# Gate sums in two parts, the rounding's integer add on VectorE, the first squares on ScalarE, and another order of the first loads in an mLSTM + squared-ReLU kernel

## The chip, the cores, the metric

One core of one Trainium2 chip. The metric is the device time of one execution in microseconds (us). Times are medians; the profile is one execution, some 2 us shorter than its time because it counts from the first to the last instruction.

## The reference, cut to what matters

```python
# 1. mLSTM cell: batch 4 x 8 heads, 768 steps, head width 40
for t in range(S):
    m_new  = maximum(f_gate[t] + m, i_gate[t])          # running maximum
    f_stab = exp(f_gate[t] + m - m_new)
    i_stab = exp(i_gate[t] - m_new);  m = m_new
    C = f_stab * C + i_stab * outer(v[t], k[t])
    n = f_stab * n + i_stab * k[t]
    y[t] = sigmoid(o_gate[t]) * (C @ q[t]) / maximum(abs(n . q[t]), 1)
# 2. y becomes x: (3072 tokens, 320)
# 3. feed-forward: w_in (320, 2048), w_out (2048, 320), given in float64
h   = maximum(x @ w_in, 0)
out = (h * h) @ w_out
```

## The kernel before

The cell is computed in 24 steps of 128 time steps (six for each batch). The gates are summed along time by scans on VectorE (`do_gates`), giving `A_sb` (sums of log f) and `i_sb` (called b). For each step, `A_bc` (the sums, spread over 128 partitions, masked on GpSimd) goes through exponentials on ScalarE into the weights `W_sb`; TensorE makes scores, VectorE multiplies them by `W_sb` (`weighted`), TensorE forms `hi`, `dC`, `hp` (`attend`), VectorE puts them together (`num`, `normalise`), and TensorE turns the rows into `xT` (`turn_rows`), the input of the feed-forward.

The weights `w_in` and `w_out` arrive as float64. Each of 26 pieces is rounded to FP32 on the chip in two steps, words on ScalarE and a join on VectorE and GpSimd:

```python
def words(self):                      # ScalarE; mag and low have two buffers each
    nc.scalar.activation(mag[:, :w], raw[:, :, 1].bitcast(F32), AF.Abs)              # L179
    nc.scalar.activation(low[:, :w], raw[:, :, 0].bitcast(U32), AF.Copy,
                         bias=2.0, scale=2.0 ** -51)                                  # L181
def join(self):                       # VectorE, and the last add on GpSimd
    nc.vector.tensor_scalar(mag, mag, ..., op0=ALU.max, op1=ALU.min)                  # L190
    nc.vector.tensor_scalar(bits, bits, scalar1=3, op0=ALU.logical_shift_left)        # L194
    nc.vector.scalar_tensor_tensor(bits, in0=self.raws[n][:, :w, 1], ...)             # L195
    nc.gpsimd.tensor_tensor(dst.bitcast(I32), bits, low.bitcast(I32), op=ALU.add)     # L199
    self.fetch()                      # the next raw piece, on the same queue as all loads
def step(self):                       # words run one piece ahead of joins
    if len(self.a) == len(self.b): self.words()
    self.words(); self.join()
```

The start, cut to the part that the argument touches (`A_bc` has two buffers, and `weigh_on(s)` issues the fetch for step s + 2):

```python
    do_gates()                        # all 768 columns at once
    ...
    rounding.words(); turn_gates(); rounding.join()
    weigh(0); transposes(1, ...); spread_A(1); scores(1, ...); weigh(1)
    weighted(0); weighted(1, spare=True)
    load(2); load_A(2)
    ...
    rounding.step(); load(3); load_A(3)
    turn_rows(0); idle(4); transposes(2); idle(4); turn_rows(1)
    rounding.step(); weigh_on(2)
```

Then steps 2 to 5 of the cell are overlapped with the first layer for the first 512 tokens, in eight turns u, each with one half group (24 matmuls, 4.5 us) on TensorE:

```python
    NEXT = (6, 8, 10, 12, 15, 18, 21, 24)      # joins done by the end of each turn
    for u in range(8):
        s = 2 + u // 2
        relu_half()
        if u % 2 == 0:
            ...                                 # scores(s), turn_rows(s-1), ffn1_half
            rounding.step(); weighted(s); weigh_on(s + 1); square_half()
        else:
            ...                                 # sigmoids where new o gates are needed
            attend(s); rounding.step(); normalise(s)
            transposes(s + 1); ffn1_half(0, u // 4, u % 4); square_half()
            ...                                 # loads
        while rounding.done < NEXT[u]: rounding.step()
```

After the loop, 497 us of the second layer and of the remaining groups follow, in which TensorE has hardly a gap (busy for 493.2 of 496.6 us).

## Time and profile before

| | before |
|---|---|
| time, median of 3 runs | 610.29 us (607.38 to 610.32) |
| profiled span, mean granted clock | 606.7 us, 0.989 |
| first half group of the first layer starts | 31.66 us |
| second half group ends (u = 0, 1) | 54.29 us |
| eighth half group ends (u = 2 to 7) | 108.53 us |
| second layer (L509) starts | 110.11 us |
| from there to the end | 496.6 us |

The five times in the middle were read from TensorE's timeline and the chain of work. They cut the span into stretches. In the profile's notation PE is TensorE, PEld its weight loads, DVE VectorE, ACT ScalarE, POOL GpSimd, SP the queue that issues the loads; "L199" is a line of the kernel. A bank is a buffer that TensorE writes its results to and that has to be read before it is filled again; a turn of the gates or of rows is their transposition by TensorE (the eight turns u of the loop are another thing). The prediction shows the lines themselves.

### The profile page before, as it was taken

How to read it: one execution, taken by the hardware profiler on the slowest of the kernel's cores; microseconds unless marked ns; L12 is line 12 of the kernel's file. 1: busy time of each engine (PE TensorE's matmuls, PEld its weight loads, DVE VectorE, ACT ScalarE, POOL GpSimd, SP SyncE). 2: the span in 40 equal slices, each digit the busy share in tenths (PEclk: the TensorE clock that was granted, in tenths of full speed). 3: DMA queues.
4: the chain of work that ended last, by engine and by line, in shares of the span. 5: the costliest groups of instructions: out<-in, count | busy, mean ns of one | idle time of the engine just before them, and what ended most of it. 6: DMA issues, size and time to landing. Idle time of an engine off the chain costs nothing.

```text
span 606.7 us, 7558 instructions
## 1 busy us (share of the span) xinstructions
PE 592.3 (98%) x2870; PEld 389.3 (64%) x2871; DVE 239.6 (39%) x468; ACT 192.4 (32%) x476; POOL 95.9 (16%) x113
## 2 busy tenths in 40 slices
PE   9979897999999999999999999999999999999997
PEld 5868776777645677645577655477755477733575
DVE  7688989712334322235323144322143431113100
ACT  3757567123351321132320524410214312022100
POOL 3345444202101110101021010101010110000000
PEclk9988998999999999999999999999999999999999
DMA  9898899615212143133143123122201000000000
GB/s 197 206 184 200 158 199 222 102 59 100 46 44 43 37 88 66 50 61 58 35 90 55 56 34 66 37 59 51 70 1 36 0 1 23 11 11 2 0 23 22
DMA packets 130901, 42.47 MB, mean 70 GB/s; under 512 B 101073, under 2 KB 127697, under 8 KB 130865
## 3 DMA queue, kind: packets, MB, share of 16 engines
q1 hardware_dynamic: 130768, 41.79, 33.2%
q8 instruction: 23, 0.38, 0.3%
q10 hardware_dynamic: 96, 0.20, 0.1%
q14 instruction: 14, 0.11, 0.1%
HBM read 37.95 MB, written 4.03 MB: 69 GB/s over the span
## 4 chain that ended last, share of the span: by engine, by line
PE 89%; DVE 6%; ACT 2%; issue 1%; POOL 1%; POOLq 0%; DVEq 0%; ACTq 0%
PE o_ps L509 35%; PE h_ps L452 23%; PE h_ps L457 7%; PE hp L392 6%; PE tp L355 3%; PE tp L342 3%; PE dC L385 3%; PE hi L378 2%; PE h_ps L476 2%; PE tp L437 1%; DVE mag L194 1%; DVE mag L195 1%; ACT W_sb L318 1%; PE idle L549 1%; POOL A_bc L312 1%
## 5 line engine op out<-in xcount | busy, mean ns | idle before, releaser
L509 PE MATMUL o_ps<-w_out,g 128*128 128x320 f32 x768 | 213.8, 435 | 0.0
L509 PEld LDWEIGHTS o_ps<-w_out,g 128*128 128x128 f32 x768 | 143.5, 190 | 57.9 <-issue 0.8
L452 PE MATMUL h_ps<-xT,w_in 128*128 128x512 f32 x320 | 146.9, 602 | 0.0
L461 DVE TENSOR_TENSOR g<-r_sb 128x512 f32<-128x512 f32 x80 | 51.7, 688 | 147.8 <-ACT r_sb L460 147.8
L452 PEld LDWEIGHTS h_ps<-xT,w_in 128*128 128x128 f32 x320 | 57.7, 190 | 69.9 <-issue 65.2
L460 ACT ACTIVATE r_sb<-h_ps 128x512 f32<-128x512 f32 x80 | 43.4, 595 | 162.6 <-PE h_ps L457 162.5
L515 ACT COPY y_sb<-o_ps 128x320 f32<-128x320 f32 x24 | 10.2, 425 | 185.8 <-PE o_ps L509 185.8
L318 ACT ACTIVATE W_sb<-A_bc,b_T 128x128 f32<-128x128 f32 x176 | 53.7, 391 | 7.9 <-POOL A_bc L312 7.9
L329 POOL TENSOR_TENSOR vw<-va,W_sb 128x328 f32<-128x328 f32 x20 | 14.9, 743 | 211.2 <-ACT W_sb L318 205.3
L367 DVE TENSOR_TENSOR P_sb<-tp,W_sb 128x512 f32<-128x512 f32 x46 | 29.6, 684 | 45.1 <-PE tp L355 43.0
L392 PE MATMUL hp<-va,P_sb 128*128 128x41 f32 x368 | 45.7, 286 | 0.0
L457 PE MATMUL h_ps<-xT,w_in 64*128 64x512 f32 x160 | 45.2, 641 | 0.0
L392 PEld LDWEIGHTS hp<-va,P_sb 128*128 128x128 f32 x368 | 44.6, 198 | 0.0
L346 DVE COPY qT<-tp 128x512 f32<-128x512 f32 x23 | 15.8, 687 | 70.2 <-PE tp L342 70.2
L411 POOL TENSOR_TENSOR C_sb<-C_sb,Cd 128x328 f32<-128x328 f32 x16 | 14.5, 906 | 138.1 <-DVE C_sb L403 137.8
L476 PE MATMUL h_ps<-xT,w_in 128*128 128x256 f32 x128 | 33.1, 415 | 3.0 <-ACT r_sb L495 1.2
L457 PEld LDWEIGHTS h_ps<-xT,w_in 64*128 64x128 f32 x160 | 12.0, 184 | 30.3 <-issue 30.3
L476 PEld LDWEIGHTS h_ps<-xT,w_in 128*128 128x128 f32 x128 | 26.1, 210 | 8.1 <-ACT r_sb L495 1.6
L355 PEld LDWEIGHTS tp<-qT,kT 40*128 40x128 f32 x384 | 24.1, 187 | 10.8 <-issue 6.8
L342 PE MATMUL tp<-ident,kq 128*128 128x128 f32 x192 | 26.6, 283 | 3.3 <-DVE num L398 3.3
L355 PE MATMUL tp<-qT,kT 40*128 40x128 f32 x384 | 27.1, 280 | 0.8 <-DVE qT L346 0.8
L342 PEld LDWEIGHTS tp<-ident,kq 128*128 128x128 f32 x192 | 23.0, 147 | 4.5 <-DVE num L398 3.8
(82 smaller groups left out, 468.8 us busy)
## 6 DMA issues: line engine op xcount, KB each, us to landing
A_bc<-a_rows SPq DMA_DIRECT2D x22, 512.0 KB, 3.9
raw<-in_moe_w_out_dram SPq DMA_DIRECT2D x16, 320.0 KB, 4.1
raw<-in_moe_w_in_dram SPq DMA_DIRECT2D x8, 512.0 KB, 5.1
kq<-in_k_dram SPq DMA_DIRECT2D x24, 160.0 KB, 4.0
kq<-in_q_dram SPq DMA_DIRECT2D x24, 160.0 KB, 4.4
va<-in_v_dram SPq DMA_DIRECT2D x24, 160.0 KB, 4.1
og<-in_o_gate_dram SPq DMA_DIRECT2D x24, 160.0 KB, 4.0
out_dram<-y_sb SPq DMA_DIRECT2D x24, 160.0 KB, 1.8
```

The costliest lines, as they stand in the source:

```text
L318: nc.scalar.activation(d["W"][:, i * n + h, :], A[i][:, h, :], AF.Exp, bias=b_T[:, b, c, i * n + h : i * n + h + 1],)
L342: nc.tensor.transpose(tp[:, j, :], d["kq"][:, i, 2 * j : 2 * j + 2, :].rearrange("p h d -> p (h d)"), ident[:],)
L355: nc.tensor.matmul(sc[i][:, j, :], lhsT=d["kT"][rows, j, :], rhs=d["qT"][rows, j, :], start=True, stop=True,)
L367: nc.vector.tensor_tensor(t, d["sc"][i], d["W"][:].rearrange("p (j two) t -> p j two t", two=2)[:, :, i, :], op=ALU.mult,)
L385: nc.tensor.matmul(dC[:, j].rearrange("p h d -> p (h d)"), lhsT=d["kq"][:, 0, 2 * j : 2 * j + 2, :].rearrange("p h d -> p (h d)"), rhs=d[" ...
L392: nc.tensor.matmul(hp[:, h, :], lhsT=d["P"][h % 2][:, h // 2, :], rhs=d["va"][:, h, :], start=True, stop=True,)
L452: nc.tensor.matmul(h[:], lhsT=w_in[:, a, fb * P : (fb + 1) * P], rhs=xT[:, a, :], start=(a == 0), stop=False,)
L457: nc.tensor.matmul(hs[i][:], lhsT=w_in2[rows, p, :], rhs=xT[rows, 2, :], start=False, stop=True)
L460: nc.scalar.activation(r[:], hs[i][:], AF.Relu)
L461: nc.vector.tensor_tensor(st["g2"][:, 2 * p + i, :], r[:], r[:], op=ALU.mult)
L476: nc.tensor.matmul(hs[i][:, n, :], lhsT=w_in[:, a, fb * P : (fb + 1) * P], rhs=xT[:, a, cols], start=(n == 0 and a == 0), stop=False,)
L509: nc.tensor.matmul(o_ps, lhsT=st["g2"][:, fb, j * P : (j + 1) * P], rhs=w_out[:, fb, :], start=(fb == 0), stop=(fb == NF - 1),)
```

## The change

Its intent: get the first gates sooner by summing 256 of 768 columns first; take the integer add off GpSimd, whose masks wait behind it; take the squares off VectorE; and order the first loads by need. Cut to its core:

```diff
-            nc.gpsimd.tensor_tensor(dst.bitcast(I32), bits, low.bitcast(I32), op=ALU.add)
+            nc.vector.tensor_tensor(dst.bitcast(I32), bits, low.bitcast(I32), op=ALU.add)
 ...
-    def do_gates():                    # scans, sums and b over all S columns
+    def do_gates(c0, c1):              # the same over columns c0*P to c1*P, carried on
+    def do_b(c0, c1):
-    def turn_gates():
+    def turn_gates(c0, c1):
 ...
-    def relu_half():                   # Relu on ScalarE, a turn later the square:
-                nc.vector.tensor_tensor(g4[:, :, i, :], r[:], r[:], op=ALU.mult)
+    def square_half():                 # Relu and square together, at the end of a turn
+                nc.scalar.activation(rs[-1][:], h[:], AF.Relu)
+                nc.scalar.activation(g4[:, :, i, :], r[:], AF.Square)
 ...
-    idle(4) ... idle(3) ... do_gates() ... turn_gates() ... weigh(0) ...
+    do_gates(0, 2); do_b(0, 2); spread_A(0); turn_gates(0, 2)
+    scores(0); weigh(0)
+    do_gates(2, NB)
+    nc.sync.dma_start(A_d[:, :], A_sb[:]); fetch(1); load_A(2)
+    rounding.words(); spread_A(1); transposes(1, (False, True))
+    weighted(0); scores(1, (True, True)); weigh(1)
+    do_b(2, NB)
+    rounding.step()
+    sigmoid(0); sigmoid(1)
+    attend(0); weighted(1, spare=True); normalise(0)
+    load(2)
+    turn_gates(2, NB)
+    attend(1)
+    rounding.step()
+    normalise(1)
+    load_o(2); load_o(3)
+    turn_rows(0); weigh_on(2); idle(4); transposes(2); turn_rows(1)
+    rounding.step()
+    load(3); load_A(3)
```

The cuts leave out the first loads (the three parts of step 0 now ahead of all raw weights), the removed idle matmuls (27 before, 16 after) and the place of `P` for step 1.

More of the change, by code (lines that the diff above doesn't have):

```diff
@@ L226, in load_gates @@
         nc.scalar.dma_start(i_sb[:], i_gate.rearrange("b h s -> (b h) s"))
-    def do_gates():
-        nc.vector.tensor_tensor_scan(m_sb[:], f_sb[:], i_sb[:], -1e30, op0=ALU.add, op1=ALU.max)
-        nc.vector.memset(f_sb[:, 0:1], 0.0)
-        nc.vector.tensor_tensor(f_sb[:, 1:], f_sb[:, 1:], m_sb[:, : S - 1], op=ALU.add)
-        nc.vector.tensor_tensor(f_sb[:, 1:], f_sb[:, 1:], m_sb[:, 1:], op=ALU.subtract)
-        nc.vector.tensor_scalar_max(f_sb[:], f_sb[:], LOG_ZERO)
+    def do_gates(c0, c1):
+        t0, t1 = c0 * P, c1 * P
+        now = slice(t0, t1)
@@ L234, in do_gates @@
         nc.vector.tensor_tensor_scan(
-            A_sb[:], keep[:].rearrange("p c t -> p (c t)"), f_sb[:], 0.0, op0=ALU.mult, op1=ALU.add,
+            m_sb[:, now], f_sb[:, now], i_sb[:, now], m_sb[:, t0 - 1 : t0] if c0 else -1e30, op0=ALU.add, op1=ALU.max,
         )
-        nc.vector.tensor_tensor(i_sb[:], i_sb[:], m_sb[:], op=ALU.subtract)
-        nc.vector.tensor_tensor(i_sb[:], i_sb[:], A_sb[:], op=ALU.subtract)
-    def turn_gates():
+        if c0 == 0:
+            nc.vector.memset(f_sb[:, 0:1], 0.0)
+            t0 = 1
@@ new lines, in do_gates @@
+        f, m = f_sb[:, t0:t1], m_sb[:, t0:t1]
+        nc.vector.tensor_tensor(f, f, m_sb[:, t0 - 1 : t1 - 1], op=ALU.add)
+        nc.vector.tensor_tensor(f, f, m, op=ALU.subtract)
+        nc.vector.tensor_scalar_max(f_sb[:, now], f_sb[:, now], LOG_ZERO)
+        nc.vector.tensor_tensor_scan(
+            A_sb[:, now], keep[:, c0:c1].rearrange("p c t -> p (c t)"), f_sb[:, now], 0.0, op0=ALU.mult, op1=ALU.add,
+        )
+    def do_b(c0, c1):
+        now = slice(c0 * P, c1 * P)
+        nc.vector.tensor_tensor(i_sb[:, now], i_sb[:, now], m_sb[:, now], op=ALU.subtract)
+        nc.vector.tensor_tensor(i_sb[:, now], i_sb[:, now], A_sb[:, now], op=ALU.subtract)
@@ L241, in turn_gates @@
+    def turn_gates(c0, c1):
         for src, dst in ((i_sb, b_T), (A_sb, eA_T)):
-            tp = ps_o.tile([P, W], F32, name="tp", tag="o_ps")[:, : S // P * BH].rearrange("p (c r) -> p c r", r=BH)
-            for c in range(NB):
-                nc.tensor.transpose(tp[:, c, :], src[:, c * P : (c + 1) * P], ident[:BH, :BH])
+            tp = ps_o.tile([P, W], F32, name="tp", tag="o_ps")[:, : (c1 - c0) * BH]
+            tp = tp.rearrange("p (c r) -> p c r", r=BH)
+            for c in range(c0, c1):
+                nc.tensor.transpose(tp[:, c - c0, :], src[:, c * P : (c + 1) * P], ident[:BH, :BH])
@@ L245, in turn_gates @@
             nc.scalar.activation(
-                dst[:].rearrange("p b c h -> p c b h"), tp.rearrange("p c (b h) -> p c b h", b=B),
+                dst[:, :, c0:c1, :].rearrange("p b c h -> p c b h"), tp.rearrange("p c (b h) -> p c b h", b=B),
                 AF.Copy if dst is b_T else AF.Exp,
@@ L362, in weighted @@
         d["P"] = []
+        if spare:
+            free = xts.tile([P, 3, W], F32, name="xT")
         for i in range(2):
-            t = ffn.tile([P, W], F32, name="r_sb", bufs=4) if spare else work.tile([P, W], F32, name="P_sb")
-            t = t[:].rearrange("p (j t) -> p j t", j=PR)
+            t = free[:, i] if spare else work.tile([P, W], F32, name="P_sb")[:]
+            t = t.rearrange("p (j t) -> p j t", j=PR)
             d["P"].append(t)
@@ L495, in relu_half @@
                 nc.scalar.activation(rs[-1][:], h[:], AF.Relu)
-            st["relu"] = rs, g4
-    def square_half():
-        if "relu" in st:
-            rs, g4 = st.pop("relu")
             for i, r in enumerate(rs):
-                nc.vector.tensor_tensor(g4[:, :, i, :], r[:], r[:], op=ALU.mult)
+                nc.scalar.activation(g4[:, :, i, :], r[:], AF.Square)
     def ffn2(g, j, part):
@@ L560 @@
     load_gates()
-    load_part(0, 0)
-    load_part(0, 1)
-    fetch(2)
+    for i in range(3):
+        load_part(0, i)
     make_consts()
-    load_part(1, 0)
-    load_part(1, 1)
-    load_part(0, 2)
+    fetch(1)
+    for i in range(3):
+        load_part(1, i)
     fetch(1)
@@ L570 @@
     load_o(1)
-    load_part(1, 2)
     fetch(1)
@@ L574 @@
     transposes(0)
-    idle(4)
+    do_gates(0, 2)
+    do_b(0, 2)
+    spread_A(0)
+    turn_gates(0, 2)
     scores(0)
-    idle(3)
-    do_gates()
-    rounding.words()
-    nc.scalar.dma_start(A_d[:, :], A_sb[:])
-    spread_A(0)
-    rounding.words()
-    turn_gates()
-    rounding.join()
-    weigh(0)
+    weigh(0)
+    do_gates(2, NB)
+    nc.sync.dma_start(A_d[:, :], A_sb[:])
+    fetch(1)
+    load_A(2)
+    rounding.words()
+    spread_A(1)
     transposes(1, (False, True))
-    spread_A(1)
+    weighted(0)
     scores(1, (True, True))
     weigh(1)
-    first.close()
-    ffn = ctx.enter_context(tc.tile_pool(name="ffn", bufs=2))
-    weighted(0)
-    weighted(1, spare=True)
-    load(2)
-    load_A(2)
+    do_b(2, NB)
+    rounding.step()
     sigmoid(0)
@@ L598 @@
     attend(0)
+    weighted(1, spare=True)
+    normalise(0)
+    load(2)
+    turn_gates(2, NB)
+    first.close()
+    ffn = ctx.enter_context(tc.tile_pool(name="ffn", bufs=2))
+    attend(1)
     rounding.step()
-    normalise(0)
+    normalise(1)
     load_o(2)
     load_o(3)
-    attend(1)
-    normalise(1)
+    turn_rows(0)
+    weigh_on(2)
+    idle(4)
+    transposes(2)
+    turn_rows(1)
     rounding.step()
@@ L607 @@
     load_A(3)
-    turn_rows(0)
-    idle(4)
-    transposes(2)
-    idle(4)
-    turn_rows(1)
-    rounding.step()
-    weigh_on(2)
     NEXT = (6, 8, 10, 12, 15, 18, 21, 24)
@@ L619 @@
         s = 2 + u // 2
-        relu_half()
         if u % 2 == 0:
@@ L631 @@
             weigh_on(s + 1)
-            square_half()
         else:
@@ L641 @@
             ffn1_half(0, u // 4, u % 4)
-            square_half()
             for r in {1: (4,), 3: (5, 6), 5: (7, 8), 7: (9,)}[u]:
@@ L651 @@
             load_o(4 + u)
-    relu_half()
-    square_half()
+        square_half()
     turn_rows(5)
```

## The prediction

> **What bounds the kernel now.** I read the page first, then the busy time of each engine in 10 us stretches, then the timeline and the chain of work up to 112 us, last who waited for whom. From the page:
>
> ```profile
> span 606.7 us, 7558 instructions
> PE 592.3 (98%) x2870; PEld 389.3 (64%) x2871; DVE 239.6 (39%) x468; ACT 192.4 (32%) x476; POOL 95.9 (16%) x113
> ...
> PE   9979897999999999999999999999999999999997
> ...
> DVE  7688989712334322235323144322143431113100
> ...
> PEclk9988998999999999999999999999999999999999
> ```
>
> One slice is 15.2 us. From slice 8 on (after about 110 us) TensorE has no gap and VectorE is at 1 to 5 tenths: 497 us that only fewer matmuls could shorten, and the change touches none. In slices 2 to 7 VectorE is at 8 to 9 tenths, TensorE has gaps, and its clock dips in two places. The stretches (columns: PE, weight loads, DVE, ACT, POOL busy, then granted clock, DMA share, GB/s):
>
> ```profile
> 30.00:40.00 10.00, 7.82 (x55) 6.21 (x53) 8.09 (x13) 5.38 (x13) 3.81 (x3) 1.00 0.74 147
> 40.00:50.00 10.00, 8.96 (x38) 8.51 (x39) 8.43 (x11) 7.88 (x20) 7.12 (x7) 0.56 0.96 242
> 50.00:60.00 10.00, 10.00 (x63) 8.07 (x61) 9.69 (x19) 6.70 (x12) 3.99 (x4) 0.93 0.95 182
> 80.00:90.00 10.00, 8.84 (x67) 7.49 (x67) 8.68 (x20) 7.84 (x19) 3.97 (x5) 1.00 0.81 190
> 100.00:110.00 10.00, 8.33 (x47) 6.50 (x47) 9.62 (x21) 4.12 (x10) 3.08 (x4) 0.83 0.89 216
> 110.00:120.00 10.00, 10.00 (x53) 7.91 (x52) 8.17 (x18) 2.85 (x7) 3.62 (x4) 1.00 0.51 75
> ```
>
> So the whole change plays between 0 and 110 us, where the second layer's matmuls (line 509) begin. Between 20.4 and 110 us the chain's own durations give TensorE this much work at full clock: eight half groups of the first layer at 4.53 us (36.2), six hp at 1.75 (10.5), five hi and five dC at 0.87 (8.7), six scores at 1.09 (6.5), four transposes at 0.9 (3.6), six row turns at 0.48 (2.9): 68 us in 89.6. The gap of 21 us is all that can be won; "faster by over 2%" needs 12.2 of it.
>
> ```profile
> 40.95 1.26 POOL L199 TENSOR_TENSOR w_in<-mag,low 128x512 int32<-128x512 int32 x1
> 41.10 1.39 DVE L190 TENSOR_SCALAR mag<-mag 128x512 f32<-128x512 f32 x1
> ...
> 54.74 0.42 DVE L190 TENSOR_SCALAR mag<-mag 128x512 f32<-128x512 f32 x1
> ...
> 90.73 0.32 DVE L190 TENSOR_SCALAR mag<-mag 128x320 f32<-128x320 f32 x1
> 90.95 0.86 POOL L199 TENSOR_TENSOR w_out<-mag,low 128x320 int32<-128x320 int32 x1 [4.66 <-DVE mag L195]
> 91.08 0.92 DVE L194 TENSOR_SCALAR mag<-mag 128x320 int32<-128x320 int32 x1
> ```
>
> The same VectorE instruction takes 0.42 us alone and 1.39 beside GpSimd's add; the shift on line 194 takes 0.33 alone and 0.92 beside it. The add that was put on GpSimd to spare VectorE costs VectorE its time anyway. The waits between 20 and 112 us (total, times, longest):
>
> ```profile
> POOL w_out L199 <- DVE mag L195: 22.5, 11, 4.7
> ...
> ACT mag L179 <- POOL w_out L199: 12.6, 6, 4.6
> ...
> ACT W_sb L318 <- POOL A_bc L312: 7.9, 5, 2.7
> ...
> PE dC L385 <- POOL vw L329: 2.7, 1, 2.7
> ```
>
> GpSimd's in-order queue sits on the add, so the masking of A_bc behind it is late, so ScalarE's exponentials are late. Once that reaches TensorE:
>
> ```profile
> 40.24 0.75 POOL vw L329
> ...
> 41.04 1.91 PE dC L385 x8
> 42.95 3.34 PE hp L392 x16
> ...
> 48.04 5.18 PE h_ps L476 x16
> ```
>
> hp takes 3.34 us here and 1.75 elsewhere: TensorE idled 2.65 us before dC and then had half its clock from about 41.2 to 51.4 us, which cost 5.1; a second spell, 102.6 to 106, cost 1.7.
>
> **What the Trainium skill says.** "SBUF — State Buffer", section "SBUF: two separate sides": VectorE and GpSimd share one port pair by an exclusive lock, held for the whole instruction, and it concerns VectorE's two-port modes and instructions with two SBUF inputs. The trace agrees: 0.42 against 1.39 us. "TensorE: Matmul & The Clock Gate", Part 1: the clock is halved after an idle window of about 3.4 us, windows that run free of the kernel, and comes back after a busy one. The trace agrees: 41.2 to 51.4 is three times 3.4, 102.6 to 106 is one. "ScalarE: Activation LUTs", "What ACT_TABLE_LOAD costs": an activation with immediates takes 186 ns + 0.833 ns an element, 613 for 512; the trace has 581 for the Relu of 128x512, so I use it for Square. The same page's "Table sets" says that cheap functions stand in every set; Square is not named there, and were it missing, table loads of 1.28 us (in this trace) would be added. "VectorE: DVE Perf Modes", "Specifications": integers are computed in FP32, exact only below 2^24, so the add becomes a rounded one; that is a matter of the result, not of time.
>
> **The change, part by part.**
> Integer add to VectorE. A piece of 512 took VectorE 0.44 + 0.46 + 0.69 = 1.6 us alone and 3.3 at worst (41.10 to 44.37); with the add, two SBUF inputs like line 502's, it takes 1.6 + 0.6 = 2.2. A piece of 320 took 1.13 alone (89.60 to 90.73), 1.71 beside an add (90.73 to 92.44); now 0.36 + 0.36 + 0.49 + 0.42 = 1.63. So VectorE's own sum hardly moves (24 pieces, 44.0 us busy by the rows of lines 190, 194 and 195 up to 112 us; 10 x 2.2 + 14 x 1.63 = 44.8 after). What is won is GpSimd: 25 us less, masks no longer late (part of the 7.9 us of ScalarE's waits), mag buffers freed sooner (17.9 us of waits on line 199, partly off the path).
>
> Squares to ScalarE. VectorE loses 16 instructions of 0.87, 13.3 us. ScalarE gains 16 at 0.5 to 0.58 start to start, about 8.5, on 58 of 90 us: 66, still under its time but no longer slack. The square now follows its Relu at once.
>
> Gates in two parts. On the path: the two sums and the first subtractions ran 4.07 to 11.97 us on 768 columns. On 256 columns a scan is some 0.6, an add 0.44, together about 3.3, so b is there at 7.4. TensorE can spread A(0) from 7.7 instead of 10.2; W(0) ends near 15 instead of 17.7. But the second part costs VectorE 4.3 + 1.4 us; its last piece, a full join (2.2) and the turn of the second part, which needs the banks of scores(1) and so weighted(1), all come before attend(1). By VectorE's new order: qT(1) near 18.5, weighted(0) to 20.3, b to 21.7, join to 23.9, C(0), weighted(1) to 25.7, normalise(0) to 27.3, num and C(1) to 28.3, join to 30.5, normalise(1) to 32.6; masking of A(2) and the sum of C(1) on GpSimd collide with that join for about 1. Row turn and copy add 1: the first half group starts near 34.2 against 31.7. **+2.5.**
>
> u = 0 and 1 of the overlapped loop (before 31.7 to 54.3). Won: W(2) is there early, so the 2.65 us stall and much of the half clock go (-2.6 each). Lost: one join fewer is done before the loop (3 against 4), so one of 2.2 falls between weighted(2) and num(2), and its words stand on ScalarE behind W(3), whose A_bc is fetched behind the third join instead of ahead of it (about 3 us later). About 5 together. **0.**
>
> u = 2 to 7 (before 54.3 to 108.5, 54.2 us in three pairs). VectorE in a pair afterwards: attention 5.2, collisions with masking and the C update about 1, joins 7.7 in the first pair and 6 x 1.63 = 9.8 in the other two: 13.9, 16, 15.5. TensorE: 2 x 4.53 + 6 = 15. The larger of the two each time: 15 + 16 + 15.5 = 46.5. The second spell of half clock should go with it. **-7.5.**
>
> First loads: v(0) before raw weights; DMA share is over 0.9 early on but nothing there ends a wait on the path, since TensorE's twelve idle matmuls run to 6.5 anyway. 0. Sum: -5.0, so 610.3 becomes **605.0 us**.
>
> **Rivals.** (1) The start really gets earlier and TensorE has no idle window, which is what dropping 11 of 27 idle matmuls suggests was intended: then the half clock goes wholly (-6.8), u = 0, 1 gains 5 and the start 1: 595 to 599. Against it: VectorE's order above, with the new wait on weighted(1). (2) A(3) late, TensorE idle for over 3.4 us before the second half group, half clock again: u = 0, 1 loses 4 more, 608 to 610. For it: the order of the fetches. (3) ScalarE becomes the bound: in a pair with sigmoids it has words 5.1, exponentials 2.65, copies 1.1, Relu and squares 4.1, table loads and sigmoids up to 4.7, 17.6 us, over TensorE's 15: about +2, 607. Against it: it no longer waits for masks.
>
> **Range and chances.** Middle 605, the rivals span 595 to 610. Eight in ten: 596.5 to 611.5. Faster by over 2% (under 598.1) needs rival 1 nearly whole: 0.17. Within 2%: 0.80. Slower (over 622) would take several new stalls at once: 0.03.
>
> **What would show it.** Line 199 on VectorE near 0.69 and 0.49 us; line 190 near 0.42 and 0.32 except beside masking. Squares on ScalarE near 0.6. The first matmul of the first layer near 34; the second half group ending near 54; line 509 starting near 103 to 105 instead of 110.0, and 497 us after it unchanged. VectorE between 54 and the end of the loop still the fullest engine. I am wrong on the start if that first matmul comes before 31, on u = 0, 1 if the clock stays at 1.00 there, on the whole if line 509 starts before 98 or after 111.

## The result, and the profile after

| | before | predicted | after |
|---|---|---|---|
| time, median of 4 runs of the same rounds | 609.07 us | 605.0 | 617.59 us (616.39 to 618.4) |
| profiled span, clock | 606.7, 0.989 | | 616.6, 0.975 |
| first half group starts | 31.66 | 34.2 (+2.5) | 38.93 (+7.3) |
| u = 0, 1 | 22.63 | 22.6 (0) | 26.82 (+4.2) |
| u = 2 to 7 | 54.24 | 46.7 (-7.5) | 52.75 (-1.5) |
| second layer starts | 110.11 | 103 to 105 | 120.07 (+10.0) |
| from there to the end | 496.6 | unchanged | 496.5 |

The ratio is 1.014, 95% interval 1.0102 to 1.0178: about 1.4% slower, so within 2% as a class, but outside the predicted range.

The page after (the clock row has one digit for each fortieth of the span, 15.4 us):

```profile
span 616.6 us, 7552 instructions
...
PE 592.4 (96%) x2859; PEld 390.8 (63%) x2860; DVE 233.1 (38%) x485; ACT 200.1 (32%) x494; POOL 68.6 (11%) x87
...
PE   9793999899999999999999999999999999999997
...
PEclk9776999799999999999999999999999999999999
```

TensorE's busy sum is what it was (592.4 against 592.3); its gaps grew. GpSimd lost 27 us, VectorE 6.5, ScalarE gained 7.7, as intended. But the fourth digit of the PE row is a 3: nearly a whole slice stands empty, and the clock row is below 9 in slices 2 to 4 and in slice 8. In stretches of 10 us (PE, weight loads, DVE, ACT, POOL busy, then clock, DMA share, GB/s):

```profile
20.00:30.00 10.00, 7.26 (x54) 6.86 (x50) 7.75 (x17) 6.93 (x14) 1.48 (x2) 0.70 0.67 120
...
50.00:60.00 10.00, 1.20 (x6) 1.21 (x7) 4.29 (x8) 7.64 (x18) 3.42 (x4) 0.57 0.46 144
...
100.00:110.00 10.00, 6.76 (x47) 5.44 (x46) 7.37 (x16) 9.97 (x25) 1.88 (x2) 0.97 1.06 208
110.00:120.00 10.00, 9.43 (x48) 7.37 (x48) 7.75 (x22) 4.95 (x11) 0.00 (x0) 0.69 0.91 190
```

Between 50 and 60 us TensorE works 1.2 us, where before it worked all ten. Between 100 and 110 ScalarE is full (9.97, before 4.12) where VectorE had been full (9.62, now 7.37). The chain of work (start, duration, what) says how the empty stretch came about:

```profile
43.95 7.13 DMA A_bc<-a_rows
...
51.26 1.06 POOL A_bc L324
...
52.95 1.84 ACT W_sb L330 x6
...
57.12 0.49 ACT r_sb L509
...
58.25 0.50 DVE num L412
...
58.80 1.97 PE tp L354 x8
```

The fetch of A_bc for step 3 is issued at 43.95 and lands 7.13 us later. Only then GpSimd masks, ScalarE takes its exponentials, and behind them in ScalarE's order come the words of two pieces (54.89 to 57.12). The joins wait for those words, `num` of step 2 stands behind a join on VectorE, and TensorE's next transposes wait for `num`. Before, the same fetch was issued at 36.04 and its mask ran at 42.17:

```profile
36.04 0.73 SPq L282 DMA_DIRECT2D A_bc<-a_rows  x1
...
42.17 1.28 POOL L312 TENSOR_SCALAR_AFFINE_SELECT A_bc<-A_bc 128x1024 f32<-128x1024 f32 x1
```

The waits between 20 and 120 us in the changed kernel (total, times, longest):

```profile
PE tp L354 <- DVE num L412: 14.3, 2, 10.5
...
POOL A_bc L324 <- DMA A_bc<-a_rows: 12.7, 1, 12.7
ACT W_sb L330 <- POOL A_bc L324: 10.0, 1, 10.0
```

One single wait of TensorE, 10.5 us, is about as long as the whole loss at the second layer's start (10.0). Why was the fetch late? In the changed start, `weigh_on(2)` comes ahead of `load_A(3)`, and `weigh_on(2)` also issues the fetch for step 4. That one went out at 35.73, and the one for step 3, needed first, stood on the load queue behind the third join's raw fetch (40.35) and three loads of step 3.

The moved operations themselves (name, shape, count, busy us, mean ns), from the groups by form up to 122 us:

```profile
L199 DVE CUSTOM_DVE_ANT_0 w_out<-mag,low 128x640 uint16<-128x640 uint16 x14 | 7.2, 515 | 2.3 <-DVE mag L195 0.5
L199 DVE CUSTOM_DVE_ANT_0 w_in<-mag,low 128x1024 uint16<-128x1024 uint16 x10 | 6.9, 693 | 1.3
```

and, on ScalarE:

```profile
L511 ACT ACTIVATE g<-r_sb 128x512 f32<-128x512 f32 x16 | 9.2, 631 | 0.0
```

The add takes 0.69 and 0.52 us on VectorE, the square 0.63 on ScalarE, and no table load stands before a square. The other three instructions of a join, for the pieces of 512, before (up to 112 us):

```profile
L195 DVE SCALAR_TENSOR_TENSOR mag<-raw,mag 128x512 int32<-128x512 int32 x10 | 8.1, 810 | 0.3
...
L194 DVE TENSOR_SCALAR mag<-mag 128x512 int32<-128x512 int32 x10 | 7.9, 789 | 0.3
...
L190 DVE TENSOR_SCALAR mag<-mag 128x512 f32<-128x512 f32 x10 | 5.9, 591 | 1.4 <-ACT mag L179 1.4
```

and after (up to 122 us):

```profile
L195 DVE SCALAR_TENSOR_TENSOR mag<-raw,mag 128x512 int32<-128x512 int32 x10 | 8.5, 846 | 0.3
...
L194 DVE TENSOR_SCALAR mag<-mag 128x512 int32<-128x512 int32 x10 | 5.8, 580 | 0.3
...
L190 DVE TENSOR_SCALAR mag<-mag 128x512 f32<-128x512 f32 x10 | 4.2, 418 | 7.2 <-ACT mag L179 7.2
```

With the pieces of 320, and counted for 24 pieces, these three lines fall from 44.0 to 38.3 us, and the add puts 14.1 on top: 52.5 us (rounded) of VectorE for the joins, where the prediction has 44.8.

### The profile page after: what moved, and what is told of

It is laid out like the page before. It is cut to its first block, busy times and chain, and to the rows that moved or that the text cites. A ratio compares the mean times of both kernels' runs of the same rounds, so it can differ in the third digit from the quotient of the medians.

```text
span 616.6 us, 7552 instructions
## 1 busy us (share of the span) xinstructions
PE 592.4 (96%) x2859; PEld 390.8 (63%) x2860; DVE 233.1 (38%) x485; ACT 200.1 (32%) x494; POOL 68.6 (11%) x87
## 4 chain that ended last, share of the span: by engine, by line
PE 91%; ACT 4%; DVE 2%; DMA 1%; issue 1%; SPq 1%; POOL 0%; POOLq 0%; DVEq 0%; ACTq 0%
PE o_ps L518 34%; PE h_ps L466 23%; PE h_ps L471 7%; PE hp L406 6%; PE tp L354 4%; PE tp L367 3%; PE h_ps L490 3%; PE hi L392 3%; PE dC L399 3%; PE tp L451 1%; DMA A_bc<-a_rows 1%; PE idle L558 1%; ACT W_sb L330 1%; PE h_ps L497 1%; PE A_ps L310 1%
## 5 line engine op out<-in xcount | busy, mean ns | idle before, releaser
L341 POOL TENSOR_TENSOR vw<-va,W_sb 128x328 f32<-128x328 f32 x20 | 15.3, 765 | 262.8 <-ACT W_sb L330 247.5
L406 PE MATMUL hp<-va,P_sb 128*128 128x41 f32 x368 | 44.1, 280 | 0.0
L406 PEld LDWEIGHTS hp<-va,P_sb 128*128 128x128 f32 x368 | 42.9, 192 | 0.0
L425 POOL TENSOR_TENSOR C_sb<-C_sb,Cd 128x328 f32<-128x328 f32 x16 | 14.1, 883 | 158.2 <-DVE C_sb L417 158.1
L367 PEld LDWEIGHTS tp<-qT,kT 40*128 40x128 f32 x384 | 24.1, 187 | 11.0 <-issue 7.2
L367 PE MATMUL tp<-qT,kT 40*128 40x128 f32 x384 | 27.1, 280 | 1.4 <-DVE qT L358 1.3
```

The lines of the kernel that those rows point to most:

```text
L367: nc.tensor.matmul(sc[i][:, j, :], lhsT=d["kT"][rows, j, :], rhs=d["qT"][rows, j, :], start=True, stop=True,)
L406: nc.tensor.matmul(hp[:, h, :], lhsT=d["P"][h % 2][:, h // 2, :], rhs=d["va"][:, h, :], start=True, stop=True,)
```

## The experiments

Eighteen kernels ran, each beside runs of the kernel before on its chip. All outputs are right. "Ratio" is always to the kernel before; the changed kernel has 1.014. Diffs are against the kernel named.

### The parts alone, in the old order

**add_dve** is the kernel before with only the add moved.

```diff
-            nc.gpsimd.tensor_tensor(dst.bitcast(I32), bits, low.bitcast(I32), op=ALU.add)
+            nc.vector.tensor_tensor(dst.bitcast(I32), bits, low.bitcast(I32), op=ALU.add)
```

> The kernel before with only the integer add moved from GpSimd to VectorE. By my sum VectorE's time for 24 pieces stays at 44 to 45 us, and the masks come sooner on GpSimd: 3 to 5 us faster, 604 to 606. Rival (VectorE is the bound up to 110 us and the add lies on it in full, 24 pieces at 0.45 to 0.65, less the collisions): 0 to 4 us slower.

Measured: 611.87 us, ratio 1.0056 (1.0037 to 1.0074). The add alone costs 3.4 us, as the rival had it. GpSimd is relieved, but the 24 joins keep VectorE busy for 52.2 us against 44.0, and what TensorE waits for, `num`, now stands behind joins that are one instruction longer. The waits between 54 and 115 us:

```profile
ACT mag L179 <- DVE w_out L199: 15.9, 8, 4.8
...
PE tp L342 <- DVE num L398: 5.4, 3, 3.3
```

TensorE's waits for `num` were 3.3 us in three times before, so they show 2.1 of the 5.0 us by which the second layer starts later in this profile (115.09); how the rest divides is not shown.

**sq_act** is the kernel before with only the squares moved, as in the change.

```diff
-    def relu_half(): ...   # Relu
-    def square_half(): ... # nc.vector.tensor_tensor(g4, r, r, op=ALU.mult), a turn later
+    def square_half(): ... # Relu and AF.Square on ScalarE, at the end of the turn
```

> The kernel before with only the squares of the first group on ScalarE, right behind their Relu. VectorE loses 13.3 us of work in 90 us; by my reasoning most of the 7.5 us that I gave u = 2 to 7 comes from this: 4 to 7 us faster, 602 to 605. Rival (ScalarE becomes the bound, its words and exponentials 1.1 us later in each of 8 steps): within 2 us of the kernel before, or slower, with the gap before the eighth half group, 2.1 us, grown to over 3.

Measured: 605.6 us, ratio 0.9954 (0.9936 to 0.9972). This is the one part that gains by itself, 2.9 us. First half group at 30.79, second layer at 107.49; u = 6, 7 still take 20.5 us.

**both_old_order** has both moves, and the start of the kernel before.

```diff
+ both diffs above; start, gates and loads as before
```

> The kernel before with both the integer add on VectorE and the squares on ScalarE, and everything else (gates in one piece, order of loads and joins) as it was. If the two parts add (+3.3 and -2.9 us measured alone): 608 to 610, so the loss of 8.5 us is the new order of the start. Rival (they feed each other: the squares make room on VectorE for the add, as I had it): 602 to 605, and the order costs 12 to 15 us.

Measured: 607.55 us, ratio 0.9989 (0.9957 to 1.0022). So the add and the squares together are worth nothing to speak of, and the rest of the change, the gates in two parts with the new order, costs some 9 us (1.014 less 0.9989, of 609 us). The loss sits in the order.

### The late fetch

**a3_early** is the changed kernel with one line moved.

```diff
     load(2)
+    load_A(3)
     turn_gates(2, NB)
 ...
     load(3)
-    load_A(3)
```

> The changed kernel with one line moved: the fetch of A(3) is issued right behind the loads of block 2, ahead of A(4), into the second buffer, which is free. Theory 1 (the 10.5 us without a matmul before the second half group, 48.3 to 58.8 us, come from the late fetch of A(3), issued at 43.95 us and landed at 51.2): the gap falls to under 3 us, TensorE keeps its clock there, and the time falls by 7 to 10 us, to 608 to 611. Rival (the join that was moved behind the exponentials of W(3) is enough by itself, whenever A(3) lands): the gap stays over 5 us and the time falls by less than 4. Line 518 would begin near 111 to 113 us against 120.1.

Measured: 610.78 us, ratio 1.0038 (1.002 to 1.0056): one moved line is worth 6.8 us by the medians, 6.2 by the ratios. The gap between the first half group's end and the second's start falls from 16.8 to 10.0 us, and the second layer starts at 111.93. TensorE's wait for `num` falls from 10.5 to 3.6 us, not quite as far as I had expected: with the transfer out of the way, the chain shows what stood behind it.

```profile
45.50 0.34 DVE mag L190
...
50.96 0.50 DVE num L412
51.46 0.04 issue
51.50 1.97 PE tp L354 x8
```

From 45.50 to 50.45 VectorE does two joins, one behind the other, ahead of `num`; TensorE waits for it. The kernel before has a join fewer in that place, since it had done one more ahead of the loop.

### The start and its clock

**idle_back** is the changed kernel with idle matmuls where TensorE waited at the second turn of the gates (23.2 to 25.6 us).

```diff
     load(2)
+    idle(10)
     turn_gates(2, NB)
+    idle(4)
```

> The changed kernel with ten idle matmuls before the turn of the second part of the gates and four behind it, where TensorE stood idle from 23.2 to 25.5 us and lost half its clock from 24.0 to 37.7. Theory (part of the late start is this half clock): granted clock 1.00 from 20 to 38 us, hp(1) in 1.9 us and not 3.55, the first half group starts 2.5 to 4 us sooner, near 35 to 36 us against 38.9. If that is handed on to the end, 614; Rival (the join and the masking on VectorE set the first half group anyway): it starts within 1 us of 38.9 and nothing is won. In both the late A(3) may take back what is won, as its fetch stands behind the third join.

Measured: 615.89 us, ratio 1.0122 (1.0105 to 1.0139). The clock stays at 1.00 to 30 us and the first half group starts 2.3 us earlier, at 36.66. But only 1 to 2 us of it reaches the end. The half clock comes at 36.6 instead and falls on the half group itself, which ends at 43.11 against 43.72; and the second half group still waits for `num` (7.9 us), behind step 3's fetch.

**a3_start** is a3_early with the first join behind the first C, the second part of b behind `normalise(0)` and `turn_gates(2, NB)` behind `normalise(1)`, so that no turn stands in TensorE's way.

```diff
-    do_b(2, NB); rounding.step()
     sigmoid(0); sigmoid(1); attend(0); weighted(1, spare=True); normalise(0)
     load(2); load_A(3)
-    turn_gates(2, NB); attend(1); rounding.step(); normalise(1)
+    do_b(2, NB); attend(1); rounding.step(); normalise(1)
+    turn_gates(2, NB); rounding.step()
```

> The changed kernel with A(3) fetched early, and in the start the first join moved behind C(1), the second part of b behind normalise(0), its turn behind attend(1). Theory (the late start comes from that join and from the turn that waits for the banks of scores(1), both ahead of attend(1)): hi(1) follows hp(0) at once, the clock stays at 1.00 to 34 us, the first half group starts at 32 to 35 us against 38.5, and the time falls by 4 to 6 us, to 605 to 607. Rival (the join and masking ahead of normalise(1) set it): it starts at 36 or later.

Measured: 609.68 us, ratio 1.0018 (0.9992 to 1.0045). The first half group starts at 34.77, 3.7 us earlier than in a3_early, yet ends only 1.7 us earlier (41.6): the clock is halved from 32.0 to 39.0 us, while TensorE first waits for `x_sb` and `xT`, and 16 of its matmuls take 5.78 us against 3.72. The second layer starts at 110.88. Of 3.7 us gained at the start, 1.1 arrived.

**a3_idle** is the changed kernel with both a3_early's line and idle_back's idle matmuls.

```diff
     load(2)
+    load_A(3)
+    idle(10)
     turn_gates(2, NB)
+    idle(4)
```

> The changed kernel with both single corrections tried before: the fetch of A(3) early (alone 1.0038 of before) and 10 + 4 idle matmuls round the second turn of the gates (alone 615.9 against 617.6, a gain of 1 to 2). Theory (the two act on separate stretches and add): clock 1.00 to 30 us, first half group at 36.5 to 37, second layer from 110 to 111, time 608.5 to 610, ratio 1.000 to 1.003. Rival (the earlier first half group only waits longer for the second, since the third join in front of num(2) decides): second layer still at 111.5 to 112.5, time 610 to 612.

Measured: 612.41 us, ratio 1.0062 (1.004 to 1.0085), no faster than a3_early (the intervals overlap), and both theories miss (the rival by 0.4 us in time and by 1.7 us on the second layer's start, 114.20). TensorE's timeline (start, busy, line, and in brackets its idle time before and what ended it):

```profile
36.09 0.44 PE L451 MATMUL tp<-ident,x_sb 128*128 128x128 f32 x2 [2.70 <-DVE x_sb L441]
...
37.98 5.30 PE L490 MATMUL h_ps<-xT,w_in 128*128 128x256 f32 x16 [0.57 <-ACT xT L452]
```

With TensorE at full clock it runs out of work earlier and waits 2.7 us for `normalise(1)` on VectorE, which stands behind a join. That join took 3.6 us (30.08 to 33.65) beside GpSimd's update of C and its mask of A_bc, and `normalise(1)` 3.4. The half clock then falls on the half group itself: 5.3 us for its first 16 matmuls, which take 3.6 to 3.7 elsewhere. The lost clock was moved, not removed, because what TensorE waits for at the start is VectorE.

### The add back on GpSimd, in the new order

**a3_pool** is a3_early with the add on GpSimd.

```diff
-            nc.vector.tensor_tensor(dst.bitcast(I32), bits, low.bitcast(I32), op=ALU.add)
+            nc.gpsimd.tensor_tensor(dst.bitcast(I32), bits, low.bitcast(I32), op=ALU.add)
```

> The changed kernel with A(3) fetched early, and the integer add back on GpSimd. If the add on VectorE costs in this order what it cost in the old one (+3.3 us): 607 to 608. If it is what frees the masks, as I had it: 612 to 615.

Measured: 609.24 us, ratio 1.0009 (0.9978 to 1.0041), 1.5 us less than a3_early's median. The intervals overlap, so this agrees in sign with add_dve and doesn't prove it again.

### The joins, and the third pair of turns

Turns u = 6, 7, from the sixth half group's end to the eighth's, take about 20 us in most kernels: 20.25 before, 20.95 after, 20.5 in sq_act, 20.6 in both_old_order, 19.75 in a3_early. Seven kernels tried what limits them, or the similar wait at `num(2)`.

**a3_wlast** puts the next step's exponentials behind joins and squares in even turns.

```diff
             weighted(s)
-            weigh_on(s + 1)
 ...
         square_half()
+        if u % 2 == 0: weigh_on(s + 1)
```

> The changed kernel with A(3) fetched early, and in the even steps the exponentials of the next block moved behind the joins and the squares. Theory (a join whose words stand behind the exponentials on ScalarE holds up num, its PSUM bank and so the transposes and the next half group): the stretch from the end of the first half group to the start of the second falls from 10.0 us to 6 to 7, that from the seventh to the eighth from 8.0 to 4 to 5, and the time by 5 to 8 us, to 603 to 606. Rival (VectorE is full, whatever ScalarE's order): under 2 us.

Measured: 614.76 us, ratio 1.0102 (1.0073 to 1.0131), 4 us worse than a3_early. The chain ahead of `num(2)` now leads through the landing of a raw piece:

```profile
44.44 5.12 DMA raw<-in_moe_w_in_dram
```

A second such wait of 3.86 us follows at 101.09. The edit moves more than the exponentials, since `weigh_on` also issues the fetch for step s + 3; which of the two delays the raw pieces was not tested.

**a3_jlate** is a3_early with joins moved from even turns, ahead of `num`, to odd ones.

```diff
-    NEXT = (6, 8, 10, 12, 15, 18, 21, 24)
+    NEXT = (4, 8, 9, 12, 13, 18, 19, 24)
```

> The changed kernel with A(3) fetched early, and with the joins that stood between weighted and num in the even steps (two, one, two, two of them) moved behind the half group of the odd steps; the number of joins in each pair stays. Theory (a join between weighted(s) and num(s), whether it waits for the exponentials or for its raw weights, holds the PSUM bank of hi and so the transposes and the next half group): end of the first half group to start of the second 10.0 to 6 to 7 us, seventh to eighth 8.0 to 4 to 5, the clock at 1.00 from 50 us on, and 6 to 9 us off 610.8: 602 to 605. Rival (VectorE is simply full): what is won there is lost in the odd steps, and the time stays within 2 us.

Measured: 621.12 us, ratio 1.02 (1.0179 to 1.0221). The gap from the first half group's end to the second's start shrinks to 5.3 us, and that from the seventh's to the eighth's to 3.7, as expected. But other turns lose more: the half group of u = 6 starts at 97.45, stops and goes on at 106.48.

```profile
106.48 3.78 PE L490 MATMUL h_ps<-xT,w_in 128*128 128x256 f32 x8 [7.14 <-ACT r_sb L509]
```

It waits for a bank that a Relu of the half group before has to read; on ScalarE that Relu (105.85) stands behind the words of the moved joins, and the last of these words waited 5.1 us for a raw piece. For its weights TensorE waits 4.0 us in all, in u = 2 and 3.

**jlate_only**, **sq_jlate** and **old_both_jlate** do nearly the same to the kernel before, to sq_act and to both_old_order.

```diff
-    NEXT = (6, 8, 10, 12, 15, 18, 21, 24)
+    NEXT = (5, 8, 9, 12, 13, 18, 19, 24)
```

> The kernel before with only these joins moved (one, one, two, two). If the same wait costs it the 2.1 us and the second spell of half clock before the eighth half group: 602 to 606. If VectorE is full: 607 to 610.

> The kernel before with the squares on ScalarE (605.6 alone) and these joins moved: 599 to 602 if the two add.

> The kernel before with add on VectorE, squares on ScalarE (607.6 together) and these joins moved: 600 to 604. If it stays above the squares with the joins moved, the add belongs on GpSimd in either order.

Measured: 615.21 (1.0095, 1.0062 to 1.0127), 612.65 (1.0066, 1.0044 to 1.0089) and 617.17 us (1.0139, 1.0111 to 1.0166): 6 to 10 us worse than their bases each time. The joins stand well where they are; delayed, they hold up the Relu (TensorE waits 5.7, 5.7 and 8.9 us for it in these three) and, less, the weights (3.1, 2.7 and 0.7).

**a3_ahead** and **sq_ahead** give `mag` and `low` a third buffer and let the words run two pieces ahead, on a3_early and on sq_act (to have the room, `Cd` and `y_sb` have one buffer).

```diff
-            mag = conv.tile([P, 512], F32, name="mag")
+            mag = conv.tile([P, 512], F32, name="mag", bufs=3)     # low likewise
 ...
     turn_rows(1)
+    rounding.words()
     rounding.step()
```

> The changed kernel with A(3) fetched early, three buffers instead of two for mag and low, and words two pieces ahead instead of one (room for it from one buffer less for Cd and y_sb). Theory (in the third pair ScalarE stands at words for a mag buffer, with Relu, squares and exponentials behind it, and the join stands at words behind the exponentials): from the end of the seventh half group to the start of the eighth 8.0 us becomes 4 to 5.5, from the first to the second 10.0 becomes 7 to 8, and the time 610.8 becomes 603 to 606. Rival (VectorE's sum of joins is the bound): the pair keeps 19 to 21 us and the time stays within 2 us.

> The same on the kernel before with the squares on ScalarE (605.6): 599 to 602 by the theory, within 2 us of 605.6 by the rival.

Measured: 612.94 (1.0065, 1.0031 to 1.01) and 606.81 us (0.9974, 0.9948 to 0.9999), against 610.78 and 605.6 of their bases. The theory that the words' buffers limit the third pair fell: it takes 20.4 and 22.7 us with a third buffer.

### A start of my own

**fill** is sq_act with the gates in two parts, but with the second b at once, two joins in the time in which VectorE waits for the first weights, the fetches of A_bc in the order of need, and the second turn behind `normalise(1)`.

```diff
+    do_gates(0, 2); do_b(0, 2); rounding.words(); spread_A(0); turn_gates(0, 2)
+    scores(0); weigh(0)
+    do_gates(2, NB); do_b(2, NB)
+    load(2); nc.sync.dma_start(A_d[:, :], A_sb[:]); load_A(2)
+    rounding.words(); rounding.join(); spread_A(1); rounding.join()
+    transposes(1, ...); weighted(0); scores(1, ...); weigh(1); load_A(3)
+    ... attend(0); weighted(1, spare=True); normalise(0) ... attend(1); normalise(1)
+    turn_gates(2, NB)
```

**fill_ahead** adds the third buffer of sq_ahead, which leaves the instructions of the start as they are in fill.

```diff
+ the diff of a3_ahead, on fill
```

> The kernel before with the squares on ScalarE, and a start of its own: gates in two parts, the second part of b at once, two joins in the time in which VectorE waits for the transposes of block 1, normalise(1) ahead of the next join, the turn of the second part behind attend(1), masking and exponentials of block 2 behind the row turn. Theory (gates in two parts win where VectorE's idle time is filled): the first half group starts at 28 to 30 us against 30.8 with the squares alone, and 603 to 605 come out. Rival (gates in two parts cost by themselves): it starts after 31.

> fill with three buffers for mag and low and words two pieces ahead. If both hold: 596 to 600, the fastest of all.

Measured: fill 605.56 us (604.98 to 613.24), ratio 0.998 (0.992 to 1.0041); fill_ahead 605.28 us with one slow execution of 614.27 left out of the ratio, 0.9945 (0.9924 to 0.9965). Executions of each fall into two groups: three near 605 and one at 613 or 614. The profile of fill caught a long one (span 611.4), that of fill_ahead a short one (603.1). From 18 to 20 us fill shows:

```profile
18.00:19.00 1.00, 0.38 (x6) 0.41 (x8) 1.00 (x3) 1.00 (x6) 1.00 (x1) 1.00 1.12 281
19.00:20.00 1.00, 1.00 (x14) 1.00 (x11) 0.67 (x2) 1.00 (x6) 0.07 (x1) 0.55 1.51 169
```

and fill_ahead:

```profile
18.00:19.00 1.00, 0.18 (x2) 0.21 (x4) 1.00 (x2) 1.00 (x5) 1.00 (x1) 1.00 1.15 262
19.00:20.00 1.00, 1.00 (x17) 0.88 (x16) 0.87 (x2) 1.00 (x6) 0.10 (x1) 1.00 1.45 162
```

The same idle time of 0.87 to 0.88 us before the scores of step 1 (L367), and in one execution the clock is halved from 19.1 to 36.1 us, in the other not at all before 40. The first half group starts at 38.73 in the one and at 30.94 in the other.

**fill_idle** puts six idle matmuls into that 0.88 us.

```diff
     transposes(1, (False, True))
+    idle(6)
     weighted(0)
     scores(1, (True, True))
```

> The start of the run called fill, whose two profiles with identical start code either kept the clock at 1.00 to 40 us or lost half of it at 19 us, with six idle matmuls more between the transposes of step 1 and its scores, where TensorE stood idle for 0.88 us. Theory (the short idle stretch near 18 us is what lets the clock fall, so the times fall into two groups near 605 and 613): TensorE's share from 17.5 to 19 us becomes 1.00, the clock stays at 1.00 at least to 30 us, the first half group starts near 31, and all timed runs lie within 2 us of 605. Rival (it is the denser work of real matmuls, or the free phase of the clock's window, and idle matmuls don't help): the times still fall into two groups more than 5 us apart, or the profile shows half the clock before 30 us.

Measured: 606.25 us (605.8 to 606.92, 5 runs), ratio 0.9958 (0.9943 to 0.9973). All five in one group. The profile:

```profile
18.00:19.00 1.00, 1.00 (x10) 0.47 (x9) 1.00 (x3) 1.00 (x6) 0.87 (x1) 1.00 1.34 205
```

TensorE's share is 1.00, the clock stays at 1.00 to 38 us, the first half group starts at 30.76. This fits the theory that the short idle stretch decided between 605 and 613, but doesn't show it: of the eight executions of fill and fill_ahead two were long, and at that rate five good ones in a row come by chance in about one case of four (0.75 to the fifth power). Its price is about 1 us against fill's three good executions (median 605.25, on another chip).

The versions that beat the kernel before are sq_act (605.6), fill_idle (606.25), in its good executions fill_ahead, and by less sq_ahead (0.9974): none by more than 0.6%, and their intervals overlap. The simplest, sq_act, is the one to keep. fill_idle against sq_act also says that gates in two parts gain nothing even in a good start: the first half group starts at 30.76 and 30.79.

## Why the prediction was wrong, by its own steps

The sum was +2.5, 0 and -7.5; the profile has +7.3, +4.2 and -1.5. The error of 15 us is made of 4.8, 4.2 and 6.0. (By the times it is 12.6: the profiles caught an execution of 608.4 before and the slowest, 618.4, after.)

**The gates in two parts, "+2.5".** The prediction's order of VectorE was right to within 0.5 us up to `normalise(0)`: qT(1) near 18.5 (18.39), weighted(0) to 20.3 (20.28), b to 21.7 (22.05), the join to 23.9 (24.4), weighted(1) to 25.7 (26.0), normalise(0) to 27.3 (27.6). The step that failed is the next, "num and C(1) to 28.3": it ended at 31.3. The prediction had counted the wait of the turn for weighted(1) on VectorE's side and not on TensorE's, which stood idle for 2.4 us and then made hi, dC and hp at half clock (hp 3.34 us). From the timeline, where hp shows with 3.55 us (3.34 in the chain of work, which leaves out the overlap):

```profile
25.56 0.60 PE L256 MATMUL tp<-ident,i_sb 32*128 32x32 f32 x4 [2.37 <-DVE xT L381]
...
30.60 3.55 PE L406 MATMUL hp<-va,xT 128*128 128x41 f32 x16
...
30.84 0.50 DVE L417 TENSOR_TENSOR C_sb<-dC,bdm 128x328 f32<-128x328 f32 x1 [1.21 <-PE dC L399]
```

Next, the join given as 2.2 took 3.65 (31.26 to 34.91) beside GpSimd's update of C and its mask, although "about 1" was set aside for that. idle_back, which kept the clock, brought 2.3 us of the 4.8; a3_start, which took the turn and a join out of the way, 3.7 against a3_early. a3_idle showed the other half of the cause: with the clock kept, VectorE still sets the start. So the half clock alone doesn't account for the whole. Rival 1, a start without half clock, did not come: the clock fell at 24.0 us.

**u = 0 and 1, "0".** The step that failed is "whose A_bc is fetched behind the third join instead of ahead of it (about 3 us later)". The order was seen, the size was wrong: 7.9 us later at the issue (43.95 against 36.04), 7.13 to landing, and 9 later at the mask. The third join ended at 41, since it inherited the late start, and three loads and step 4's fetch stood ahead as well. a3_early shows that this costs 6.8 us. The prediction had this as its rival 2 ("608 to 610"); it happened, together with a start that was late by itself, which no rival joined to it. The other terms are confirmed: for "one join fewer is done before the loop", two joins stand ahead of `num` in a3_early's chain, and the 2.65 us stall before `dC` of step 2, counted as won, is gone from the timeline after.

**u = 2 to 7, "-7.5".** The first two pairs were right: 15 and 16 predicted, 15.3 and 16.5 measured. The third, "15.5", took 20.95. The step that failed is "the larger of the two each time": it took the pair as bound by VectorE's or TensorE's sum. In the trace the third pair is one chain from engine to engine: words, Relu and square, a table load of 1.28 us, eight exponentials, words again, all on ScalarE without a pause (9.97 of 10 us), then join and `num` on VectorE, then TensorE, which loses its clock in the wait:

```profile
99.02 0.50 ACT mag L179
...
103.07 1.28 ACT L330
...
104.36 2.28 ACT W_sb L330 x8
...
106.92 0.39 ACT mag L179
...
110.10 0.42 DVE num L412
...
110.57 1.12 PE tp L354 x4
```

Rival 3, ScalarE as the bound, came true here in part; but the pair is as long with the squares on VectorE (20.25 before, with VectorE at 9.62 of 10), so relieving one engine moved the wait to another. Later joins, a third buffer and later exponentials all failed to shorten it, each for another reason. It is shortest in fill_ahead, fill and fill_idle (18.4, 18.6 and 19.4); why was not tested. That stays open.

**What held.** The add's 0.69 and 0.49 us (0.69 and 0.52), the squares' 0.6 (0.63), no extra table load, line 190 faster without GpSimd (591 to 418 ns for 512 columns), line 194 too (789 to 580), the unchanged 497 us after the loop. That "the add becomes a rounded one" has no support in the trace: it appears as a custom instruction on twice as many uint16 elements, and results were correct; exactness was not tested.

**The add, "VectorE's own sum hardly moves".** This step failed too. The prediction set rows of busy time, collisions included (44.0 us), against a sum of undisturbed costs, 2.2 and 1.63 us for a piece (44.8). Measured in the same rows, a piece takes 2.54 and 1.94 us and the 24 joins 52.5 (52.2 in add_dve). Without GpSimd's add, lines 190, 194 and 195 save 5.7 us, not the 14.1 that the add costs; line 195 got no faster (810 to 846 ns). Of the 13.3 us that the squares free on VectorE, this takes back 8.5, and the whole profile shows only 6.5 less on VectorE. A smaller slip: the list of TensorE's work counts four transposes where the timeline has five (at 28.86, 46.09, 64.28, 82.66 and 98.94), so the gap is 20 us and not 21.

**What is shown and what is argued.** Shown by an edit: the order costs about 9 us (both_old_order), the fetch 6.8 of the 617.6 (a3_early), the squares gain 2.9, the add costs 3.4 in the old order. "The order" is all that both_old_order leaves out, the gates in two parts, the first loads and the removed idle matmuls included; none of these was run alone. Argued: that the short idle stretch decides the clock in fill (fill_idle agrees). Not shown: how the remaining 2 to 3 us of the order split between the half clock at the start and the additional join, because the kernels that changed one shifted the other.

## What to carry to other kernels

Order the fetches on one queue by when their data are needed, and look for calls that issue a fetch as a side effect; here the fetch for step 3 stood behind the one for step 4, a join's raw fetch and three loads, and that cost 1.1%. Price an operation moved to another engine by that engine's busy rows before and after, both with collisions or both without, and by what then stands behind it in that engine's order: here the sum grew by 8.5 us where the prediction had 0.8. When a wait on TensorE is shortened, check where the clock falls next: in idle_back, a3_idle and a3_start the half clock moved on to the first half group.

## What the Trainium skill lacked or had wrong

- "TensorE: Matmul & The Clock Gate", Part 1, ties the half clock to an idle window of about 3.4 us. No such window stands before several falls here: in the kernel before TensorE had just stood idle for 2.65 us when the clock fell near 41.2, in the changed kernel for 0.8 us (24.0), in fill for 0.88 us a little earlier (19.1; the same stretch cost fill_ahead's profile nothing). In the 3.4 us before the last two, TensorE was busy for 2.60 and 2.52 us by the profile. Part 1 does name short idles between groups of matmuls as a cause of a swinging clock, but gives no length or share. What exactly is counted, these runs don't tell.
- "VectorE: DVE Perf Modes", Specifications, says that integers are computed in FP32. It doesn't say that an int32 add of two tensors can be carried out by a custom instruction on twice as many uint16 elements, as in the changed kernel, in 693 ns for 128x512 and 515 ns for 128x320, about what an FP32 product of two tensors takes (684 ns for the 128x512 squares in add_dve).
